# An attention kernel with a mixture-of-experts tail: q and k transposes placed apart between score steps, the two heads of a pair attended apart, the loads of the start and of V rearranged

## Chip, cores and metric

One core of a Trainium2 chip. The metric is the time on the device in microseconds (us) of one execution, lower is better. A profiled execution shows a span, from its first to its last instruction, about 2 us below that time. Single executions of this kernel spread by 2 to 3% (207.68 to 212.74 us before the change). A run is called slow when it is over 1.5% above the fastest of the same kernel, and verdicts use the fast runs; a verdict is "unclear" when the interval of the ratio includes a change of 2%.

## The reference

Causal attention over 64 (batch, head) groups, with 16 unmasked "beacon" keys and values ahead of the 576 tokens, then a soft mixture of experts on the result. Cut to what matters:

```python
B, H, S, Nb, D = 8, 8, 576, 16, 64
k_all = concat([beacon_k, k], axis=2); v_all = concat([beacon_v, v], axis=2)
scores = q @ k_all^T / sqrt(D)           # causal on the 576, beacons open
a = softmax(scores)
x = (a @ v_all)  ->  [4608, 512]
logits = x @ phi                         # 32 slots
slot_input = softmax over tokens(logits).T @ x
slot_out[e] = relu(slot_input[e] @ w1[e]) @ w2[e]      # 8 experts
out = softmax over slots(logits) @ slot_out
```

## The kernel before

The work goes over 32 pairs of heads, four pairs a batch. For each pair PE (matmul) transposes q and k into `qT`, `kT`. It makes the scores in four steps and ACT (ScalarE) turns each into exp. POOL (GpSimd) masks the diagonal. PE attends (exp times V), and DVE (VectorE) normalizes. V of a batch arrives as rows in `vbuf`, which has two buffers, and DVE turns it into `vh` with two stream transposes. The tail (logits of the last batch, experts, output) takes about 50 us. POOL issues the loads that cast to f16: V in four quarters, the beacon V rows on top of the first quarter, and the expert weights. The queue of SP (SyncE) issues q and k.

In the traces here each engine takes up its work in the order of the program (below, DVE stands idle for 3.68 us ahead of a V transpose, with a q copy behind it whose transposes PE has finished), so where a piece stands in the loop body decides what waits behind it. Four small pieces of the mixture of experts are spread over the pairs too: `xt_piece` transposes the attended result into `xT`, `logit_piece` multiplies it by phi and ACT takes exp, `dt_piece` transposes those exps into `dT`, and `add_si` adds to the slot inputs. They use the same two transpose buffers `tr`. The body for pair `n` (`b`, `g` are its batch and its place in it), cut:

```python
def transp(n):                      # 18 + 18 PE transposes, each 18 into one of TWO tr buffers
    for (f, dst) in ((qf, qT[n % 3]), (kf, kT[n % 3])):
        tp = ps_tr.tile([P, J, 64], BF, name="tr", tag="tr")
        ...                         # PE transposes
        nc.vector.tensor_copy(out=dst..., in_=tp...)       # DVE frees tr
def stage(m): transp(m); load_pair(m + 5)

for n in range(NP):
    score(n, 0); score(n, 1)
    ...                             # starts of pairs 0 and 1 cut
    xt_piece(n - 2); attend(n - 1)  # attend: both heads, 30 matmuls, then normalize on DVE
    score(n, 2)
    stage(n + 2)                    # q and k transposes together
    score(n, 3)
    if g == 1: logit_piece(b - 1, 0)                       # and (b - 1, 1) for g == 2,
    ...                                                    # dt_piece g == 3, add_si g == 0
    if b >= 1 and b < B - 1 and g >= 2:
        turn_v(b + 1, g - 2)        # DVE: half of the next batch's V transpose
    if n >= 4 and b + 2 < B:
        load_v(b + 2, g)            # a quarter of V
        if g == 3: load_bv(b + 2)   # its 16 KB of beacon V, over quarter 0
    want = ... 14 * (n - 2) // 15 ...                      # weight loads
```

The softmax here doesn't subtract the row's maximum and nothing guards it: scores larger than these inputs give would overflow.

## Time and profile before

Three runs gave a median of 209.36 us (207.68 to 212.74). The profiled span is 205.7 us. From the timeline of ACT I read when the first exp of each pair starts, which divides the span:

| stretch | us |
|---|---|
| start, to the first exp of pair 6 | 40.4 |
| pairs 6 to 31 (first exp to first exp), 25 periods | 115.7, that is 4.63 each |
| from there to the end | 49.6 |

The page of the kernel before: busy time by engine, then three rows of 40 equal slices (granted PE clock in tenths, busy share of the DMA engines in tenths, GB/s landed).

```profile
span 205.7 us, 7788 instructions
...
PE 153.0 (74%) x3409; PEld 113.3 (55%) x3409; DVE 134.7 (65%) x278; ACT 126.8 (62%) x188; POOL 93.6 (46%) x184
...
PEclk9999999999999969999997899999999999999755
DMA  5999979699999999999999999999999920079996
GB/s 177 328 222 353 255 225 242 116 243 248 259 261 255 260 265 262 259 263 256 261 341 267 261 294 267 251 246 215 212 213 208 213 56 3 0 304 409 419 422 280
```

No engine is full, but the DMA row stands at 9 from about 40 us until 165. V and weights land as f16, half their bytes in memory, so the GB/s row understates what is read (the page counts 50.88 MB moved, but 62.69 MB read from memory and 9.44 MB written).

The waits of the kernel before over the whole span (who waited for whom: us in total, times, longest us); the prediction quotes them between 30 and 150 us, where they are a little smaller:

```profile
ACT ex L263 <- PE sc L257: 29.7, 29, 4.7
...
ACT eLh L324 <- PE tr L320: 8.5, 12, 0.8
...
PE tr L320 <- DVE qT L245: 6.8, 11, 0.7
...
PE tr L332 <- DVE qT L245: 3.7, 6, 0.8
```

ACT waits for PE. PE waits where a logits or a dT piece needs one of the two transpose buffers while DVE still copies q and k, one behind the other.

The 16 KB of beacon V, line of the source query, with the time from issue to landing:

```profile
L146 POOL DMA_DIRECT2D vbuf<-in_beacon_v_dram x7: 521/521/552, 25.3 to 124.0; - x7
...
DMA to landing us min/median/max: 3.3/6.7/9.2
```

And this is where it stands in time for batch 4, in the timeline (start us, us, engine, line, what): issued by POOL during pair 11, used by DVE at the end of pair 14.

```profile
66.33 0.52 POOL L146 DMA_DIRECT2D vbuf<-in_beacon_v_dram  x1
...
81.31 0.75 DVE L245 COPY kT<-tr 128x576 bf16<-128x576 bf16 x1
...
81.97 1.14 DVE L135 STREAM_TRANSPOSE vh<-vbuf 128x512 f32<-128x512 f32 x1
...
82.97 1.11 DVE L135 STREAM_TRANSPOSE vt<-arena 96x512 f32<-96x512 f32 x1
```

The load is issued 15.6 us ahead of the V transpose that needs it. No V transpose waits in the loop.

### The profile page before, as it was taken

The page shows a single profiled execution, that of the slowest core. Times are in us where ns is not written, and L with a number is a line of the kernel's source. Part 1 is how long each engine was busy: PE and PEld are TensorE (multiplying, and loading weights), DVE is VectorE, ACT ScalarE, POOL GpSimd, SP SyncE. Part 2 cuts the span into 40 slices and gives each one's busy share as a digit, 9 for nine tenths or more (in the row PEclk, how much of TensorE's full clock was granted, in tenths as well). Part 3 has the DMA queues.
Part 4 walks back from the last instruction along what each step waited for, and adds up shares of the span by engine and source line. Part 5 has one row for each costly group of instructions (what it writes and reads, how often), then busy time and mean ns, then how long its engine had stood idle before and what let it go on. Part 6 is the DMA issues. An engine that isn't in the chain of part 4 may idle for free.

```text
span 205.7 us, 7788 instructions
## 1 busy us (share of the span) xinstructions
PE 153.0 (74%) x3409; PEld 113.3 (55%) x3409; DVE 134.7 (65%) x278; ACT 126.8 (62%) x188; POOL 93.6 (46%) x184
## 2 busy tenths in 40 slices
PE   2654798888778698878887987888878998788100
PEld 1433676667656586756666666667656664333000
DVE  4507969679658858976794689678655541299300
ACT  2560578588677658858884787688679122299200
POOL 5657372868675644644583467445457000000000
PEclk9999999999999969999997899999999999999755
DMA  5999979699999999999999999999999920079996
GB/s 177 328 222 353 255 225 242 116 243 248 259 261 255 260 265 262 259 263 256 261 341 267 261 294 267 251 246 215 212 213 208 213 56 3 0 304 409 419 422 280
DMA packets 20273, 50.88 MB, mean 247 GB/s; under 512 B 5392, under 2 KB 5392, under 8 KB 19216
## 3 DMA queue, kind: packets, MB, share of 16 engines
q0 software_dynamic: 8000, 21.75, 54.1%
q1 hardware_dynamic: 12096, 28.35, 38.2%
q8 instruction: 26, 0.43, 0.8%
q10 hardware_dynamic: 144, 0.29, 0.4%
q14 instruction: 7, 0.06, 0.1%
HBM read 62.69 MB, written 9.44 MB: 351 GB/s over the span
## 4 chain that ended last, share of the span: by engine, by line
PE 38%; DVE 36%; DMA 8%; issue 7%; ACT 2%; POOL 2%; DVEq 0%; ACTq 0%; POOLq 0%
PE av L284 12%; DVE xb L295 9%; DVE qT L245 8%; PE sc L257 7%; DMA vbuf<-in_v_dram 5%; DVE arena L569 5%; DVE vh L135 4%; PE tr L320 4%; PE tr L309 4%; DVE kT L245 4%; DMA vbuf<-in_beacon_v_dram 2%; PE tr L243 2%; DVE r L294 2%; PE av L537 2%; PE tr L343 2%
## 5 line engine op out<-in xcount | busy, mean ns | idle before, releaser
L263 ACT ACTIVATE ex<-sc 128x1024 f16<-128x1024 f32 (+1 forms) x124 | 100.8, 871 | 30.2 <-PE sc L257 29.7
L265 POOL TENSOR_SCALAR_AFFINE_SELECT ex<-ex 128x1024 f16<-128x1024 f16 x31 | 34.0, 1096 | 51.6 <-ACT ex L263 51.6
L257 PE MATMUL sc<-qT,kT 64*128 64x128 bf16 (+5 forms) x576 | 42.7, 255 | 4.2 <-issue 1.3
L284 PE MATMUL av<-vh,ex 128*128 128x65 f16 x868 | 37.1, 200 | 1.2 <-DVE vh L135 0.6
L284 PEld LDWEIGHTS <-ex 128*128 128x128 f16 x930 | 35.8, 109 | 2.6 <-issue 2.3
L243 PE MATMUL tr<-idb,arena 64*64 64x64 bf16 x1152 | 28.2, 202 | 10.3 <-DVE qT L245 5.0
L243 PEld LDWEIGHTS <-arena 64*64 64x64 bf16 x1152 | 23.9, 116 | 18.1 <-issue 15.9
L295 DVE TENSOR_TENSOR xb<-av,r 128x640 f16<-128x640 f32 (+1 forms) x33 | 26.5, 804 | 1.1
L257 PEld LDWEIGHTS <-kT 64*128 64x128 bf16 (+1 forms) x576 | 19.5, 99 | 12.9 <-issue 7.5
L245 DVE COPY qT<-tr 128x576 bf16<-128x576 bf16 x32 | 23.9, 748 | 2.4 <-PE tr L243 2.2
L245 DVE COPY kT<-tr 128x576 bf16<-128x576 bf16 x32 | 24.0, 749 | 1.4 <-PE tr L243 1.4
L313 DVE COPY xT<-tr 128x592 f16<-128x592 f16 x32 | 14.4, 455 | 12.9 <-PE tr L309 12.8
L135 DVE STREAM_TRANSPOSE vh<-vbuf 128x512 f32<-128x512 f32 x16 | 18.1, 1134 | 6.8 <-DMA arena<-in_v_dram 6.8
L164 POOL DMA_DIRECT2D arena<-in_moe_w_dram x32 | 17.6, 552 | 0.1
L111 POOL DMA_DIRECT2D vbuf<-in_v_dram x28 | 15.7, 566 | 3.5 <-DVE xT L313 3.5
L294 DVE RECIPROCAL r<-av 128x10 f32<-128x10 f32 (+1 forms) x33 | 7.2, 218 | 15.1 <-PE av L284 15.1
L320 PE MATMUL tr<-xT,phih 128*128 128x288 f16 x56 | 9.1, 284 | 6.9 <-DVE qT L245 6.8
L309 PE MATMUL tr<-idh,xb 128*128 128x128 f16 (+1 forms) x160 | 13.9, 220 | 0.3 <-DVE xb L295 0.3
L569 DVE TENSOR_SCALAR arena<-fp,rc 128x512 f32<-128x512 f32 x18 | 12.3, 746 | 0.7 <-PE fp L565 0.7
L565 PE MATMUL fp<-soh,eLh 128*128 128x512 f16 x36 | 10.5, 377 | 2.6 <-ACT arena L567 1.4
L567 ACT ACTIVATE arena<-fp,rc 128x512 f32<-128x512 f32 x18 | 11.3, 685 | 1.7 <-PE fp L565 1.0
L309 PEld LDWEIGHTS <-xb 128*128 128x128 f16 (+1 forms) x160 | 9.2, 98 | 5.5 <-issue 4.8
(83 smaller groups left out, 135.6 us busy)
## 6 DMA issues: line engine op xcount, KB each, us to landing
arena<-in_moe_w_dram POOLq DMA_DIRECT2D x32, 512.0 KB, 10.2
arena<-in_q_dram SPq DMA_DIRECT2D x32, 288.0 KB, 10.1
arena<-in_k_dram SPq DMA_DIRECT2D x31, 288.0 KB, 12.2
out_dram<-arena SPq DMA_DIRECT2D x8, 1024.0 KB, 8.5
vbuf<-in_v_dram POOLq DMA_DIRECT2D x31, 128.0 KB, 7.3
out_dram<-arena SPq DMA_DIRECT2D x2, 512.0 KB, 3.1
arena<-in_v_dram POOLq DMA_DIRECT2D x4, 128.0 KB, 9.9
arena<-in_k_dram ACTq DMA_DIRECT2D x1, 288.0 KB, 2.8
```

The costliest lines, as they stand in the source:

```text
L135: nc.vector.transpose(out=dst[:, e], in_=src.bitcast(FP).rearrange("p (j e) -> p e j", j=TK)[:, e])
L164: nc.gpsimd.dma_start(out=arena[:, wloc[m]:wloc[m] + WP], in_=src)
L243: nc.tensor.transpose(tp[po:po + 64, j, :], hi, idb[po:po + 64, po:po + 64])
L245: nc.vector.tensor_copy(out=dst[:, Nb:Nb + S].rearrange("p (s j) -> p s j", j=J), in_=tp[:, :, :].rearrange("p j s -> p s j"))
L257: nc.tensor.matmul(sc[0:kn, a, col:col + un], kT[n % 3][64 * a:64 * a + 64, P * c:P * c + kn], qT[n % 3][64 * a:64 * a + 64, u0:u0 + un], ...
L263: nc.scalar.activation(ex[n][:, :, o:o + w], sc[:, :, 0:w], AF.Exp, scale=scale)
L265: nc.gpsimd.affine_select(out=ex[n][:, :, 0:512].rearrange("p a (c t) -> p a c t", c=4), in_=ex[n][:, :, 0:512].rearrange("p a (c t) -> p ...
L284: nc.tensor.matmul(av[0:m, a, i * DD:(i + 1) * DD], ex[n][0:kn, a, o:o + m], vchunk(b, 2 * g + a, c, kn), start=(c == 0), stop=(c == i))
L295: nc.vector.tensor_tensor(out=xo[:, z], in0=avv[:, z, :, 0:D], in1=r_.unsqueeze(3).broadcast_to([P, z.stop - z.start, NCH, D]), op=AL.mult)
L309: nc.tensor.transpose(tp[:, i, 0:m], xb[b % 2][0:m, i, 2 * g:2 * g + 2, :].rearrange("p h d -> p (h d)"), idh[0:m, 0:m])
L320: nc.tensor.matmul(lp[:, 0:w], phih[:, t, :, :].rearrange("p g s -> p (g s)"), xT[b][:, t, Nb + hf * w:Nb + (hf + 1) * w], start=(t == 0), ...
L569: nc.vector.tensor_scalar(out=osb[:, j, :], in0=fp_[:, :], scalar1=rc[:, i:i + 1], scalar2=None, op0=AL.mult)
```

## The change

The intent: spread PE's work evenly between score steps, so that ACT never waits long for a score. q is transposed between steps 1 and 2 and k between 2 and 3; one head is attended ahead of step 2 and the other behind step 3. The V transposes move up to between steps 0 and 1. At the start, later loads are held back so that the first V lands sooner. V and beacon V loads from batch 3 on come later, and so do most weight loads. The exp tile's layout changes too. The core of the diff, cut:

```diff
+    def hold(n):                       # a tiny DVE write that delays the load over it
+        o = lend + 2 * (n % QKS) * 2 * J * D
+        nc.vector.memset(arena[0:1, o:o + 2], 0.0)
 ...
-    load_pair(2)
-    load_pair(3)
-    nc.sync.dma_start(out=bkf[:, 1:B, :], in_=bks[:, 1:B, :])
-    load_pair(4)                       # these now behind hold(2), and hold(3) at the end of pair 0
-    double_beacons(nc.gpsimd, 1, 0, 1) # now on DVE
 ...
     for n in range(NP):
         score(n, 0)
+        if n == 1:
+            turn_v(0, 0)
+        if n in (3, 4):
+            turn_v(1, n - 3)
+        if 1 <= b < B - 1 and g >= 2:
+            turn_v(b + 1, g - 2)
         score(n, 1)
-            attend(n - 1)
+        if m < NP:
+            transp(m, 0)                # q
+            attend_head(n - 1, 0)
+                xt_piece(x)
         score(n, 2)
-            stage(n + 2)
+            transp(m, 1)                # k
         score(n, 3)
+            attend_head(n - 1, 1)
+            normalize(n - 1)
 ...
-        if n in (3, 4):
-            turn_v(1, n - 3)
-        if b >= 1 and b < B - 1 and g >= 2:
-            turn_v(b + 1, g - 2)
-        if n >= 4 and b + 2 < B:
-            load_v(b + 2, g)
-            if g == 3:
-                load_bv(b + 2)
+        if n >= 5:
+            x, y = divmod(n - 5, 4)
+            if x + 3 < B:
+                load_v(x + 3, y)
+            if y == 0 and 3 <= x + 2 < B:
+                load_bv(x + 2)          # at the end of the pair just before its V transpose
-        want = 0 if n < 3 else 14 * (n - 2) // 15 if n < 24 else 19 + 7 * (n - 23) // 4
+        want = 7 * max(n - 1, 0) // 10 if n < 24 else 16 + 9 * (n - 23) // 5
```

More of the change, by code (lines that the diff above doesn't have):

```diff
@@ L67 @@
                 if u0 <= lo < u0 + un:
-                    blk[(c, i)] = soff[st] + col + lo - u0
+                    blk[(c, i)] = (2 * soff[st] + col + lo - u0, width[st])
     assert len(blk) == 15
@@ L178 @@
     load_pair(1)
-    load_pair(2)
-    load_pair(3)
-    nc.sync.dma_start(out=bkf[:, 1:B, :], in_=bks[:, 1:B, :])
-    load_pair(4)
     phif = const.tile([P, NDC, NSL], FP, name="phif")
-    nc.sync.dma_start(out=phif[:, :, :], in_=moe_phi.rearrange("(c p) e -> p c e", p=P))
     idb = const.tile([P, P], BF, name="idb")
@@ L233, in beacons, with transp @@
                     "p b (g r n) -> p (b g) r n", g=H // 2, r=2)[:, :, r, :])
-    def transp(n):
-        (nc.vector if n < 2 else nc.gpsimd).tensor_copy(out=kT[n % 3][:, 0:Nb], in_=bkT[:, n, :])
-        for (f, dst) in ((qf, qT[n % 3]), (kf, kT[n % 3])):
-            t = f.pop(n)
-            tp = ps_tr.tile([P, J, 64], BF, name="tr", tag="tr")
-            for j in range(J):
-                for po in (0, 64):
-                    hi = t[po:po + 64, j, :].bitcast(BF)[:, 1::2]
-                    nc.tensor.transpose(tp[po:po + 64, j, :], hi,
-                                        idb[po:po + 64, po:po + 64])
-            nc.vector.tensor_copy(out=dst[:, Nb:Nb + S].rearrange("p (s j) -> p s j", j=J),
-                                  in_=tp[:, :, :].rearrange("p j s -> p s j"))
+    def transp(n, i):
+        if i == 1:
+            (nc.vector if n < 2 else nc.gpsimd).tensor_copy(out=kT[n % 3][:, 0:Nb],
+                                                            in_=bkT[:, n, :])
+        t = (qf, kf)[i].pop(n)
+        tp = ps_tr.tile([P, J, 64], BF, name="tr", tag="tr")
+        for j in range(J):
+            for po in (0, 64):
+                hi = t[po:po + 64, j, :].bitcast(BF)[:, 1::2]
+                nc.tensor.transpose(tp[po:po + 64, j, :], hi, idb[po:po + 64, po:po + 64])
+        nc.vector.tensor_copy(
+            out=(qT, kT)[i][n % 3][:, Nb:Nb + S].rearrange("p (s j) -> p s j", j=J),
+            in_=tp[:, :, :].rearrange("p j s -> p s j"))
     ex = {}
@@ L251, in score @@
         if st == 0:
-            ex[n] = (arena[:, 20 * WP:20 * WP + 2 * EW].rearrange("p (a w) -> p a w", a=2)
-                     if n == 2 else exq.tile([P, 2, EW], F16, name="ex", tag="ex"))
+            ex[n] = (arena[:, 20 * WP:20 * WP + 2 * EW] if n == 2 else
+                     exq.tile([P, 2 * EW], F16, name="ex", tag="ex"))
         sc = scs[st % 2]
@@ L261, in score @@
                     start=True, stop=True)
-        w, o = width[st], soff[st]
-        nc.scalar.activation(ex[n][:, :, o:o + w], sc[:, :, 0:w], AF.Exp, scale=scale)
+        w = width[st]
+        e = ex[n][:, 2 * soff[st]:2 * soff[st] + 2 * w].rearrange("p (a w) -> p a w", a=2)
+        nc.scalar.activation(e, sc[:, :, 0:w], AF.Exp, scale=scale)
         if st == 0:
-            nc.gpsimd.affine_select(
-                out=ex[n][:, :, 0:512].rearrange("p a (c t) -> p a c t", c=4),
-                in_=ex[n][:, :, 0:512].rearrange("p a (c t) -> p a c t", c=4),
-                compare_op=AL.is_ge, fill=0.0, base=0,
-                pattern=[[0, 2], [0, 4], [1, P]], channel_multiplier=-1)
@@ L270, in score @@
-        if st == 1:
-            nc.gpsimd.affine_select(
-                out=ex[n][0:UL, :, o:o + UL], in_=ex[n][0:UL, :, o:o + UL],
-                compare_op=AL.is_ge, fill=0.0, base=0,
-                pattern=[[0, 2], [1, UL]], channel_multiplier=-1)
-    def attend(n, split=False):
-        b, g = divmod(n, H // 2)
-        for a in range(2):
-            for i in range(NCH):
-                m = P if i < 4 else UL
-                for c in range(i + 1):
-                    kn = P if c < 4 else UL
-                    o = blk[(c, i)]
-                    nc.tensor.matmul(
-                        av[0:m, a, i * DD:(i + 1) * DD],
-                        ex[n][0:kn, a, o:o + m],
-                        vchunk(b, 2 * g + a, c, kn),
-                        start=(c == 0), stop=(c == i))
+            e4 = e.rearrange("p a (c t) -> p a c t", c=4)
@@ new lines, in score, with attend_head @@
+            nc.gpsimd.affine_select(out=e4, in_=e4, compare_op=AL.is_ge, fill=0.0, base=0,
+                                    pattern=[[0, 2], [0, 4], [1, P]], channel_multiplier=-1)
+        if st == 1:
+            e1 = e[0:UL, :, 0:UL]
+            nc.gpsimd.affine_select(out=e1, in_=e1, compare_op=AL.is_ge, fill=0.0, base=0,
+                                    pattern=[[0, 2], [1, UL]], channel_multiplier=-1)
+    def attend_head(n, a):
+        b, g = divmod(n, H // 2)
+        for i in range(NCH):
+            m = P if i < 4 else UL
+            for c in range(i + 1):
+                kn = P if c < 4 else UL
+                o, w = blk[(c, i)]
+                nc.tensor.matmul(
+                    av[0:m, a, i * DD:(i + 1) * DD],
+                    ex[n][0:kn, o + a * w:o + a * w + m],
+                    vchunk(b, 2 * g + a, c, kn),
+                    start=(c == 0), stop=(c == i))
@@ L289, in attend, with normalize @@
+    def normalize(n, split=False):
+        b, g = divmod(n, H // 2)
         r5 = sml.tile([P, 2, NCH], FP, name="r5", tag="r5")
@@ L353, in add_si, with load_more @@
         nc.vector.tensor_tensor(out=z, in0=z, in1=sp, op=AL.add)
-    def stage(m):
-        transp(m)
+    def load_more(m):
         if m + 5 < NP:
             load_pair(m + 5)
-    double_beacons(nc.vector, 0, 0, 1)
+    for r in range(2):
+        double_beacons(nc.vector, r, 0, 1)
     beacons(0, 1)
-    stage(0)
+    transp(0, 0)
+    transp(0, 1)
+    hold(2)
+    load_pair(2)
     nc.vector.tensor_copy(out=idh[:, :], in_=idb[:, :])
@@ L367 @@
         score(n, 0)
-        score(n, 1)
-        if n == 0:
-            stage(1)
-        elif n == 1:
-            turn_v(0, 0)
-            stage(2)
+        if n == 1:
[4 more added lines that the diff above has]
+            turn_v(b + 1, g - 2)
+        if 13 <= n < 15:
+            turn_tail(1, n - 13)
+        score(n, 1)
+        m = n + 1 if n < 4 else n + 2
+        if m < NP:
+            transp(m, 0)
+        if n in (2, 3):
+            attend_head(n - 2, 0)
+        elif n > 3:
+            attend_head(n - 1, 0)
+        if n >= 3:
+            for x in {3: (0,), 4: (1, 2)}.get(n, (n - 2,)):
+                xt_piece(x)
+        score(n, 2)
+        if n == 3:
+            beacons(1, B)
+        if m < NP:
+            transp(m, 1)
+            if n > 0:
+                load_more(m)
+        score(n, 3)
+        if n == 0:
+            hold(3)
+            load_pair(3)
+            nc.sync.dma_start(out=bkf[:, 1:B, :], in_=bks[:, 1:B, :])
+            load_pair(4)
+            nc.sync.dma_start(out=phif[:, :, :], in_=moe_phi.rearrange("(c p) e -> p c e", p=P))
+            load_more(0)
+            load_more(1)
+        if n == 1:
             turn_v(0, 1)
@@ L376 @@
             turn_tail(0, 1)
-            for r in range(2):
-                double_beacons(nc.gpsimd, r, 1, B)
-        elif n <= 3:
-            attend(n - 2)
-        else:
-            for m in ((n - 2,) if n > 5 else (2 * n - 8, 2 * n - 7)):
-                xt_piece(m)
-            attend(n - 1)
-        score(n, 2)
-        if n == 2:
-            beacons(1, B)
-        if 2 <= n < NP - 2:
-            stage(n + 2)
-        score(n, 3)
-        if n == 1:
-            stage(3)
-        if n == 3:
-            attend(2)
-        if n >= 5 and g == 1:
-            logit_piece(b - 1, 0)
-        if n >= 6 and g == 2:
-            logit_piece(b - 1, 1)
+        if n in (2, 3):
+            attend_head(n - 2, 1)
+            normalize(n - 2)
+        elif n > 3:
+            attend_head(n - 1, 1)
+            normalize(n - 1)
+        if n == 3:
+            attend_head(2, 0)
+            attend_head(2, 1)
+            normalize(2)
+            transp(5, 0)
+            transp(5, 1)
+            load_more(5)
         if n >= 6 and g == 3:
             dt_piece(b - 1)
+        if n >= 5 and g in (1, 2):
+            logit_piece(b - 1, g - 1)
         if n >= 8 and g == 0:
@@ L405 @@
         if n == 1:
+            for r in range(2):
+                double_beacons(nc.gpsimd, r, 1, B)
             for qd in range(4):
@@ L420 @@
                 load_v(2, qd)
-        if n >= 4 and b + 2 < B:
-            load_v(b + 2, g)
-            if g == 0 and b == 1:
-                load_bv(2)
-            if g == 3:
-                load_bv(b + 2)
+        if n == 4:
+            load_bv(2)
+        if n >= 5:
[4 more added lines that the diff above has]
+                load_bv(x + 2)
         if 8 <= n < 11:
             load_tail(1, n - 8)
-        if 13 <= n < 15:
-            turn_tail(1, n - 13)
-        want = 0 if n < 3 else 14 * (n - 2) // 15 if n < 24 else 19 + 7 * (n - 23) // 4
+        want = 7 * max(n - 1, 0) // 10 if n < 24 else 16 + 9 * (n - 23) // 5
         while wl < min(want, NPC):
@@ L434 @@
             wl += 1
+    while wl < NPC:
+        load_w(wl)
+        wl += 1
     G = 4
@@ L461 @@
     xt_piece(NP - 2)
-    attend(NP - 1, split=True)
+    attend_head(NP - 1, 0)
+    attend_head(NP - 1, 1)
+    normalize(NP - 1, split=True)
     lps = [scs[0][:, hf, 0:S // 2] for hf in range(2)]
```

## The prediction

> **What bounds it now.** Three unprofiled runs give a median of 209.36 us (207.68 to 212.74); the profiled span is 205.7. First exp of each pair in the timeline: pair 2 at 20.2, pair 6 at 40.4, pair 31 at 156.1. So start-up is 40 us, then 25 pairs at 4.63 us, then 50 us of tail that the change hardly touches. In the pair loop no engine is full: ACT needs 3.5 us a pair (exps 3.15, logits 0.3); DVE about 3.7 (q and k copies 0.7 each, normalize 1.04, xT 0.45, half a V transpose 0.55, small ones); PE back to back about 3.7 (scores 1.05, attend 1.2, transposes 0.68, xT 0.26, logits, slots). PE's order paces it: in the waits between 30 and 150 us ACT waits 23.3 us for scores and 8.5 for logits, PE 13 us for the transpose buffers that DVE's q and k copies free, and several "issue" stalls of over 1 us. The windows show a DMA share of 1.03 to 1.08 from 40 to 165 us: V and weight loads land 6 to 12 us after issue.
>
> **The change** removes and adds no arithmetic. It moves half the attend and half the transposes into other gaps between score steps: PE's longest stretch without a score falls from 1.45 us (xT plus attend) to about 1.2, and the k copy no longer queues directly behind the q copy, so the 0.65 us wait of each logits group and 0.5 of each dT group should mostly go. I work out 3.8 to 4.05 us a pair, plus 0.2 for issue stalls and throttle: 4.2. Over 25 pairs: -11 us.
>
> Start-up: V of batch 0 landed only at 16.4 us, and DVE idled 6.8 us before its first V transpose. Holding pair 2 and later back, and freeing POOL of the beacon cast, should land V near 10 us: -5. But batch 1's V beacons are now needed at the start of pair 3, not its end (before: issued 25.3, landed 30.4, on the chain). I keep -2.5 us.
>
> Added wait: from batch 3 on, a batch's beacon V is issued one pair before its V transpose (three before), behind a V load in the same queue. It leaves POOL 0.6 to 1 us before DVE wants it, yet the trace lands these 16 KB loads 3.35 to 9.2 us after issue. DVE stalls there with all copies behind it, five times. The Trainium skill (DMA: Bandwidth & Descriptors, Anatomy of one DMA) gives about 2 us fixed cost; the trace's least is 3.35. Fewer early weight loads (7 in ten pairs, before 14 in 15) shorten the queue. I charge 1.5 us net each: +7.5; it could be 3.
>
> All issuers share 16 DMA engines (same page, Issuing engines are not separate DMA queues; the share above 1 agrees); 62.7 MB read at about 410 GB/s forbids much under 190 us.
>
> Sum: 209.4 - 11 - 2.5 + 7.5 = about 203 us; 8 in 10 between 195 and 212. Chances: faster 0.54, same 0.32, slower 0.14.
>
> **What would show it.** Pair period 4.1 to 4.3 where no V transpose waits; PE's waits for transpose buffers under 5 us; first V transpose at 10 to 11 us; V transposes waiting 2 to 4 us for beacon V at pairs 3, 10, 14, 18, 22, 26; last weights landing without holding the experts.
>
> **What would make it wrong.** Beacon V landing faster in an emptier queue (then 192 to 196), each stall costing its full 3 to 5 us (then 210 or more), or DVE becoming the bound through V transposes ahead of the q copy.

## The result and the profile after

The changed kernel takes 237.06 us (234.92 to 237.53, 4 runs). The ratio to the kernel before is 1.1354, 95% interval 1.1247 to 1.1460. A ratio here is the mean time of one kernel's fast runs over that of the other's fast runs of the same rounds, so it is not quite the ratio of the quoted medians. The forecast of 203 us, with 212 as its upper end, was wrong.

The profiled spans, divided as before:

| stretch | before | after | difference | predicted |
|---|---|---|---|---|
| start, to the first exp of pair 6 | 40.4 | 47.8 | +7.4 | -2.5 |
| pairs 6 to 31 | 115.7 | 135.6 | +19.9 | -3.5 (-11 and +7.5) |
| from there to the end | 49.6 | 51.5 | +1.9 | 0 |
| span | 205.7 | 234.9 | +29.2 | -6 |

Of the +1.9 us at the end, 1.2 lie in the last pair itself, where the second head is now attended behind the last score step; the rest was not followed up.

The page after, with the line of the chain that ended last:

```profile
span 234.9 us, 7781 instructions
...
PE 169.6 (72%) x3409; PEld 123.4 (53%) x3409; DVE 139.0 (59%) x281; ACT 126.9 (54%) x188; POOL 93.4 (40%) x183
...
PEclk9999999999795997699769955995599999999955
DMA  6899729999999899779949983999999999029996
GB/s 203 188 337 344 182 57 173 252 263 228 260 208 225 202 246 182 181 191 220 208 110 224 248 192 104 203 229 211 188 179 208 194 212 197 8 101 416 419 423 250
...
DMA vbuf<-in_beacon_v_dram 14%; PE av L280 13%; PE sc L256 9%; PE tr L242 8%; ACT ex L263 4%; DVE vh L139 4%; DVE arena L597 3%; DVE qT L243 3%; DMA arena<-in_beacon_k_dram 3%; DMA vbuf<-in_v_dram 3%; PE tr L319 2%; PE tr L308 2%; DVE xb L294 2%; POOL ex L266 2%; PE av L565 2%
```

Busy times of ACT and POOL are as before, and DVE has 4 us more. What grew is idle time and PE's busy time at a lower clock: the clock row, nearly all 9 before, now has a group of 5 to 7 every 20 us or so. And the chain spends 14% of the span on a 16 KB load.

The waits after, over the whole span:

```profile
ACT ex L263 <- PE sc L256: 60.7, 32, 6.0
...
DVE vh L139 <- DMA vbuf<-in_beacon_v_dram: 24.9, 5, 5.8
PE tr L242 <- DVE qT L243: 24.9, 7, 6.1
...
DVE vh L139 <- DMA arena<-in_v_dram: 3.9, 2, 3.2
```

DVE waits 24.9 us for beacon V in five places (one at the start, four in the loop), plus once 3.2 us (pair 10) that the trace puts down to the V tail's load. The landing times say that this wait too ends with beacon V: in all five loop pairs that load lands 0.1 to 0.5 us before the V transpose starts (69.28 and 69.47 us in pair 10). PE's wait for DVE's q copy is, by chance, also 24.9 us. ACT's wait for scores rises from 29.7 to 60.7. The load itself has not become slower, as its source query shows:

```profile
L150 POOL DMA_DIRECT2D vbuf<-in_beacon_v_dram x7: 537/549/549, 25.8 to 154.3; - x7
...
  DVE vh L139: 24.9, 5
...
DMA to landing us min/median/max: 3.6/5.1/7.0
```

Before, 3.3 to 9.2 us from issue to landing; now 3.6 to 7.0. What changed is when it is wanted. The same batch 4 as above, in the timeline after:

```profile
86.53 0.54 POOL L150 DMA_DIRECT2D vbuf<-in_beacon_v_dram  x1
...
87.09 0.82 DVE L294 TENSOR_TENSOR xb<-av,r 128x640 f16<-128x640 f32 x1
...
89.03 0.37 PE L256 MATMUL sc<-qT,kT 64*128 64x464 bf16 x2
...
91.59 1.12 DVE L139 STREAM_TRANSPOSE vh<-vbuf 128x512 f32<-128x512 f32 x1 [3.68 <-DMA vbuf<-in_beacon_v_dram]
92.58 1.07 DVE L139 STREAM_TRANSPOSE vt<-arena 96x512 f32<-96x512 f32 x1
93.50 0.73 DVE L243 COPY qT<-tr 128x576 bf16<-128x576 bf16 x1
...
94.29 0.69 PE L242 MATMUL tr<-idb,arena 64*64 64x64 bf16 x18 [4.89 <-DVE qT L243]
...
95.20 1.00 PE L280 MATMUL av<-vh,ex 128*128 128x65 f16 x14
95.31 0.52 ACT L263 ACTIVATE ex<-sc 128x416 f16<-128x416 f32 x1 [4.81 <-PE sc L256]
```

Read it downwards. POOL issues the load at 86.5. DVE is done with normalize at 87.9 and wants the V transpose at once, 1.4 us after the issue instead of 15.6. It starts at 91.59, 3.68 us idle. The q copy is behind it, and behind another transpose. PE did its q transposes, half an attend, xT and score step 2 (89.03), and then stands before the k transposes. These need one of the two transpose buffers, and the q copy has to free it: 4.89 us idle. ACT gets no score for 4.81 us. When PE resumes, 18 transposes take 0.69 us and 14 attend matmuls 1.00; the same groups of 18 and 14 took 0.47 and 0.63 at 87.77 and 88.17. Two windows show why, the first being this pair (us, busy us and instructions of PE, PEld, DVE, ACT, POOL, then granted clock, DMA share, GB/s), the second the next three pairs:

```profile
core 0: us, PE busy (x) PEld busy (x) DVE busy (x) ACT busy (x) POOL busy (x), PEclk, DMA share, GB/s
87.75:97.88 10.13, 5.24 (x95) 3.92 (x93) 5.48 (x9) 3.76 (x7) 2.57 (x5) 0.67 0.97 201
97.88:109.57 11.69, 11.43 (x300) 8.96 (x296) 9.88 (x21) 10.06 (x14) 7.64 (x15) 1.00 0.75 172
```

The granted clock is 0.67 in the stalled pair and 1.00 after it. The Trainium skill (TensorE: Matmul & The Clock Gate, Part 1) says that PE falls to half clock after an idle window of about 3.4 us and needs about as long busy to get back. The trace agrees in part: its clock records show 0.5 six times ahead of the output phase, once for 3.4 us and five times for 6.8 or 10.2 us. These five begin 1.8 to 3.8 us after PE went idle in each of the five stalls and end 3.7 to 6.5 us after PE resumed (here from 91.2 to 98.0). A whole idle window was not needed: the sixth record, at 60.4 us, and two in the kernel before, at 73.5 and 111.1, follow 3.4 us in which PE was busy for 2.23, 1.79 and 1.79 us and never idle for more than 1.4 at a time.

The five pairs that hold such a wait (10, 14, 18, 22, 26) last 8.69, 10.13, 9.83, 11.31 and 10.90 us, together 50.9; before, the same five took 22.8. The other twenty pairs take 84.7 us, 4.24 each; before, 92.9, or 4.65 each. So the loop lost 28.0 us in five pairs and won 8.2 in twenty. Counted as the prediction's sum counts, against the 4.24 us of the other pairs, the five cost 29.7 us more, 5.9 each.

### The profile page after: what moved, and what is told of

It reads as the page before. It is cut to its first block, busy times and chain, and to the rows that moved or that the text cites. A ratio compares the mean times of both kernels' runs of the same rounds, so it can differ in the third digit from the quotient of the medians.

```text
span 234.9 us, 7781 instructions
## 1 busy us (share of the span) xinstructions
PE 169.6 (72%) x3409; PEld 123.4 (53%) x3409; DVE 139.0 (59%) x281; ACT 126.9 (54%) x188; POOL 93.4 (40%) x183
## 4 chain that ended last, share of the span: by engine, by line
PE 43%; DMA 21%; DVE 15%; ACT 5%; issue 4%; POOL 4%; DVEq 1%; SPq 0%; ACTq 0%
DMA vbuf<-in_beacon_v_dram 14%; PE av L280 13%; PE sc L256 9%; PE tr L242 8%; ACT ex L263 4%; DVE vh L139 4%; DVE arena L597 3%; DVE qT L243 3%; DMA arena<-in_beacon_k_dram 3%; DMA vbuf<-in_v_dram 3%; PE tr L319 2%; PE tr L308 2%; DVE xb L294 2%; POOL ex L266 2%; PE av L565 2%
## 5 line engine op out<-in xcount | busy, mean ns | idle before, releaser
L263 ACT ACTIVATE ex<-sc 128x1024 f16<-128x1024 f32 (+1 forms) x124 | 100.3, 871 | 61.9 <-PE sc L256 60.7
L242 PE MATMUL tr<-idb,arena 64*64 64x64 bf16 x1152 | 35.0, 211 | 29.6 <-DVE qT L243 24.9
L242 PEld LDWEIGHTS <-arena 64*64 64x64 bf16 x1152 | 28.8, 123 | 43.9 <-issue 34.8
L256 PE MATMUL sc<-qT,kT 64*128 64x128 bf16 (+5 forms) x576 | 46.6, 277 | 4.3 <-ACT ex L263 1.7
L280 PE MATMUL av<-vh,ex 128*128 128x65 f16 x868 | 43.9, 208 | 0.3
L280 PEld LDWEIGHTS <-ex 128*128 128x128 f16 x930 | 40.3, 115 | 5.5 <-issue 1.6
L139 DVE STREAM_TRANSPOSE vh<-vbuf 128x512 f32<-128x512 f32 x16 | 18.1, 1130 | 28.8 <-DMA vbuf<-in_beacon_v_dram 24.9
L243 DVE COPY kT<-tr 128x576 bf16<-128x576 bf16 x32 | 24.2, 757 | 10.0 <-PE tr L242 9.8
L256 PEld LDWEIGHTS <-kT 64*128 64x128 bf16 (+1 forms) x576 | 21.3, 108 | 15.4 <-issue 8.1
L312 DVE COPY xT<-tr 128x592 f16<-128x592 f16 x32 | 14.7, 459 | 7.5 <-PE tr L308 6.2
L308 PE MATMUL tr<-idh,xb 128*128 128x128 f16 (+1 forms) x160 | 15.2, 231 | 1.5 <-DVE xb L294 0.9
L115 POOL DMA_DIRECT2D vbuf<-in_v_dram x28 | 15.6, 560 | 0.0
L308 PEld LDWEIGHTS <-xb 128*128 128x128 f16 (+1 forms) x160 | 11.1, 107 | 2.0 <-DVE xb L294 1.3
L319 PE MATMUL tr<-xT,phih 128*128 128x288 f16 x56 | 11.7, 341 | 0.0
```

The lines of the kernel that those rows point to most:

```text
L139: nc.vector.transpose(out=dst[:, e], in_=src.bitcast(FP).rearrange("p (j e) -> p e j", j=TK)[:, e])
L242: nc.tensor.transpose(tp[po:po + 64, j, :], hi, idb[po:po + 64, po:po + 64])
L243: nc.vector.tensor_copy(out=(qT, kT)[i][n % 3][:, Nb:Nb + S].rearrange("p (s j) -> p s j", j=J), in_=tp[:, :, :].rearrange("p j s -> p s j"))
L256: nc.tensor.matmul(sc[0:kn, a, col:col + un], kT[n % 3][64 * a:64 * a + 64, P * c:P * c + kn], qT[n % 3][64 * a:64 * a + 64, u0:u0 + un], ...
L263: nc.scalar.activation(e, sc[:, :, 0:w], AF.Exp, scale=scale)
L280: nc.tensor.matmul(av[0:m, a, i * DD:(i + 1) * DD], ex[n][0:kn, o + a * w:o + a * w + m], vchunk(b, 2 * g + a, c, kn), start=(c == 0), sto ...
```

## The experiments

Theory A: the beacon V load, issued one pair ahead and wanted right behind normalize, makes the loss of the loop. Rival B: the new order of PE and DVE is itself bad (V transposes ahead of the q copy, attend in halves), and another wait would take the place of this one. Four kernels on one chip, where the kernel before took 209.07.

**e1_bv_early**: the changed kernel, beacon V issued two pairs earlier, all else kept.

```diff
-            if y == 0 and 3 <= x + 2 < B:
-                load_bv(x + 2)
+            if y == 2 and x + 3 < B:
+                load_bv(x + 3)
```

> The changed kernel with one edit: from batch 3 on, the beacon V of a batch is issued two pairs earlier (three pairs ahead of its V transpose, as before the change); everything else stays. Theory A (the late beacon V is the loss of the pair loop: five pairs of 8.7 to 11.3 us against about 4.2): those five pairs fall to 4.2 to 5.2 us, the last V quarter still being issued one pair ahead; time 208 to 214 us against 237, so within 2% or slightly over the kernel before. Rival B (the new order on PE and DVE is what costs, and another wait takes the place of this one): still over 225 us.

Measured: 215.61 us, ratio 1.0298 (1.0235 to 1.0360). One moved 16 KB load takes most of the loss away. It is 1.6 us over what I gave it: in three of the five pairs the V transpose still waits 1.2 to 1.8 us, now that the last V quarter is the late one (issued two pairs ahead, not one as I had written; for pair 10 at 57.6 us, landed at 65.1, wanted at 63.9), and pairs 10 and 14 still take 7.0 and 7.6 us.

**e2_v_as_before**: the V quarters also one pair earlier, so the V load timing of before.

```diff
-        if n >= 5:
-            x, y = divmod(n - 5, 4)
-            if x + 3 < B:
-                load_v(x + 3, y)
-            if y == 0 and 3 <= x + 2 < B:
-                load_bv(x + 2)
+        if n >= 4 and b + 2 < B:
+            load_v(b + 2, g)
+            if g == 3:
+                load_bv(b + 2)
```

> The changed kernel with the whole V load timing of before from batch 3 on (V quarters one pair earlier, beacon V two pairs earlier). Theory A: as e1 or 1 to 3 us better, 206 to 212 us, with no V transpose waiting for a DMA after pair 6, and the pair period 4.0 to 4.3. What is left over the kernel before is then the start, where the first exp of pair 6 is 7.5 us later. Rival B: over 225 us.

Measured: 211.79 us, ratio 1.0094 (1.0008 to 1.0179). No V transpose waits after pair 6. The pair period of 4.0 to 4.3 us did not come: it is 4.52 here and 4.48 in s3 below. (The profile of e2 fell in a slow run, so I take sizes of the loop from s3, which is fast.)

**e3_turn_late**: the late loads kept, the V transposes back at the end of the pair.

```diff
         score(n, 0)
-        if 1 <= b < B - 1 and g >= 2:
-            turn_v(b + 1, g - 2)
 ...     # behind attend, normalize, logits, dT:
+        if 1 <= b < B - 1 and g >= 2:
+            turn_v(b + 1, g - 2)
```

> The changed kernel with its late V and beacon V loads, but the V transposes from batch 2 on back at the end of the pair, behind normalize, where they stood before. Theory A: beacon V lands 5 to 7 us after issue and now has about 4 us more, so the five waits shrink from 5 us to 1 to 2 us and stand behind the q, k and xT copies: 211 to 219 us. Rival B: over 225 us.

Measured: 214.10 us, ratio 1.0220 (1.0151 to 1.0289). Two of the waits are left, 0.7 and 1.6 us, and the loop takes 112.5 us instead of 135.6.

**e4_before_bv_late**: the kernel BEFORE with only these two pieces put in.

```diff
         score(n, 0)
+        if b >= 1 and b < B - 1 and g >= 2:
+            turn_v(b + 1, g - 2)
         score(n, 1)
 ...
-            if g == 3:
-                load_bv(b + 2)
+        if b >= 2 and g == 1 and b + 1 < B:
+            load_bv(b + 1)
```

> The kernel BEFORE, with only the two pieces that theory A blames put in: beacon V issued one pair ahead from batch 3 on, and the V transposes from batch 2 on between the first two score steps. Transposes, attend, start and weights stay as before. Theory A: 20 to 30 us slower than before (229 to 239 us), with five pairs of 9 to 11 us. Rival B: within 4 us of before.

Measured: 236.34 us, ratio 1.1248 (1.1144 to 1.1353), almost the whole loss of the change, in the old kernel. The same five pairs take 12.7, 10.3, 10.1, 10.0 and 6.8 us (the last below my 9 to 11, the first above). The whole loss is in the loop, 141.3 us instead of 115.7, while start and end are as before. The trace names beacon V as the releaser of two of the five waits only, but in all five the load lands 0.02 to 0.2 us before the V transpose starts. The timeline of DVE in this run has the same line:

```profile
90.97 1.12 DVE L135 STREAM_TRANSPOSE vh<-vbuf 128x512 f32<-128x512 f32 x1 [4.83 <-DMA vbuf<-in_beacon_v_dram]
```

What follows: A holds and B falls, in both directions. Either edit taken back (e1, e3) gives most of the time back, because each alone leaves the load a lead of 5.0 us or more, from its issue to the moment when DVE wants it; the two together leave 1.2 to 2.1 us in the changed kernel and 0.8 to 1.8 in e4. The new exp layout and weight timing were not taken apart, but e1 to e3 keep the layout and the weight timing, and their loops are no longer than before (112.5 to 114.6 us against 115.7).

Next, the start, 7.4 us later than before. Theory H: the holds. Theory T: batch 1's V transpose, now ahead of the copies of pair 3, waits for its beacon V with the work of that pair behind it. The timeline of DVE in the changed kernel shows that wait:

```profile
29.56 1.13 DVE L139 STREAM_TRANSPOSE vh<-vbuf 128x512 f32<-128x512 f32 x1 [5.76 <-DMA vbuf<-in_beacon_v_dram]
```

This load is late in itself: POOL issues it at 25.8 us, about 2 us after DVE wants it, having stood idle for 2.3 us until a V load landed, and it lands 3.7 us after issue.

Before, the first exps of pairs 3 and 4 came at 26.0 and 30.5 us; in the changed kernel at 24.2 and 39.0. So pair 3 came 1.7 us earlier and then lost 10.3. The holds are not shown to have brought it forward: without them it comes at 23.3 (s1, s3), and e4, with the start of before, has it at 24.7. Three kernels on another chip, where before took 211.42. All start from e2.

**s1_no_hold**: without the holds.

```diff
+    load_pair(2); load_pair(3); bkf load; load_pair(4); phif load      # at once, as before
-    hold(2); load_pair(2)
-            hold(3); load_pair(3); bkf load; load_pair(4); phif load
```

> The kernel of e2 (V load timing of before) and also the q, k, beacon and phi loads of the start issued at once as before, without the two holds. Theory H (the holds cost the start: pair 2 lands at 13.4 us, and the k beacons, which POOL must cast before it issues batch 1's V, only at 18.1 us): the first exp of pair 6 comes 3 to 6 us earlier than the 47.7 us of e2, time 206 to 209 us. Theory T (what costs is the V transpose of batch 1 put ahead of the copies of pair 3, with DVE idle 5.8 us and the work of three pairs behind it): within 2 us of e2, 210 to 213 us.

Measured: 211.98 us, ratio 1.0003 (0.9904 to 1.0102). The first exp of pair 6 is at 47.1, against 47.7 in e2. The holds do bring the first V transpose forward (14.7 us here, 11.2 in the changed kernel), but nothing was gained by it at pair 6. DVE's waits in the first 40 us still have the line:

```profile
DVE vh L139 <- DMA vbuf<-in_beacon_v_dram: 5.1, 1, 5.1
```

**s2_turn1_late**: holds kept, batch 1's two V transposes back at the end of pairs 3 and 4.

```diff
         score(n, 0)
-        if n in (3, 4):
-            turn_v(1, n - 3)
 ...     # end of the pair
+        if n in (3, 4):
+            turn_v(1, n - 3)
```

> The kernel of e2 with batch 1's two V transposes back at the end of pairs 3 and 4, holds kept. Theory T: pair 4's first exp moves from 38.9 to 31 to 34 us, time 204 to 208 us. Theory H: little change, 210 to 213 us.

Measured: 208.89 us, ratio 0.9870 (0.9795 to 0.9945); pair 4 begins at 33.4 instead of 38.9, pair 6 at 43.9 instead of 47.7. So T holds for 5.5 us at pair 4 and 3.8 at pair 6, about half of the 7.4 us; the rest goes with the edits of s3 and s4 below. The time is 0.9 us above my range, and the verdict against the kernel before is unclear by the 2% rule.

**s3_both**: both edits.

> The kernel of e2 with both start edits. If both theories hold in part, 202 to 206 us, faster than before by 1.5 to 3%; the loop stays at 4.4 to 4.55 us a pair because pauses for PE instructions (gaps of about 1 us ending some 1.4 us after an instruction packet, 15 us in the loop of e2, 7 before) eat what the order gains. If only the loop of e2 counts and neither start edit does: 210 to 213 us.

Measured: 207.64 us, ratio 0.9809 (0.9725 to 0.9892), a little above the range I gave in us, on a chip where the kernel before was slower too; by the 2% rule this is unclear as well. Pair 4 begins at 32.0, pair 6 at 42.5. With and without holds the intervals overlap (s1 and e2, s3 and s2), so what the holds cost or save is not settled; it is 2 us at most in these medians.

**c1_warm_in_wait**, same chip: the changed kernel with dummy matmuls where PE waits, to see what the fallen clock is worth.

```diff
+        if 2 <= b < B - 1 and g == 2:
+            for _ in range(45):                       # into unused columns of av
+                nc.tensor.matmul(av[:, 0, NCH * DD:512], idh[:, :],
+                                 xT[b - 1][:, 0, 0:512 - NCH * DD], start=True, stop=True)
         if m < NP:
             transp(m, 1)
```

> The changed kernel with 45 dummy matmuls of 187 columns (about 4 us) put on PE just ahead of the k transposes of the five pairs in which PE waits for DVE, writing unused columns of the attend banks. Nothing else changes. Theory C (part of each loss is PE's granted clock falling to 0.5 while it waits and for about 3 us after: 18 transposes 0.69 instead of 0.47 us, half an attend 1.00 instead of 0.63): the clock stays at 1.0 there, and each such pair is 1 to 1.5 us shorter, 229 to 233 us. If the clock plays no part, or DVE sets the pace after the wait: 236 to 239 us.

Measured: 231.38 us, ratio 1.0987 (1.0872 to 1.1103) against 1.1354 for the changed kernel: more matmuls, less time. The window of pair 14 of this run (columns as above) has the clock at 1.00:

```profile
87.02:94.56 7.54, 7.54 (x140) 6.45 (x138) 4.87 (x8) 3.68 (x7) 2.57 (x5) 1.00 0.99 216
```

The five pairs take 43.6 us instead of 50.9. In this profile DVE's waits before them sum to 20.8 us instead of 22.3, so 1.5 of the 7.3 us are not the clock's; the rest is about 1.2 us a stall, an average over pairs that differ: they are 0.7 to 2.6 us shorter, DVE waited only 1.9 us in the pair shown, and the clock stayed at 1.00 in four of the five (in pair 22 it fell to 0.5 for 3.4 us). The low clock of the changed kernel lasted 3.7 to 6.5 us after PE resumed, longer than the 3 us of the expectation.

Last, where the gain of the new order goes once the stalls are gone. In s3 the loop takes 112.1 us, 3.6 less than before, and not the 11 that I had forecast. The PE timeline of e2 shows a kind of gap that waits for nothing that the profile shows:

```profile
107.03 0.22 PE L308 MATMUL tr<-idh,xb 128*128 128x128 f16 x1
108.56 0.38 PE L308 MATMUL tr<-idh,xb 128*128 128x128 f16 x4 [1.30 <-issue]
```

In the middle of five equal transposes PE stops for 1.3 us. The trace also has the packets of the queue that carries instructions, 16 KB each, and one ended at 107.00. I counted gaps of PE's weight loads of 0.35 us or more that end 1.1 to 1.7 us behind the end of such a packet: 8 with 7.6 us in pairs 6 to 31 before, 13 with 12.5 us in s3, and 1 with 1.3 us in the changed kernel, whose stalls presumably leave PE time to be supplied. (e2's profile is of a slow run, but s3, with the thirteen, is fast.) Theory F: those packets come late because the DMA engines are crowded by weights, q, k and V. Two kernels, one look each (state unknown), with all weight loads issued behind the loop; the results are still correct, only the loop is to be compared.

**d1_s3_weights_after** and **d2_before_weights_after**:

```diff
-        want = ...
+        want = 0                    # in the kernel before: the weight loop moved behind the pair loop
```

> The kernel of s3 with all 32 weight loads issued after the pair loop (still correct; the whole must get some 60 to 80 us longer, only the loop counts). Theory F (in s3 thirteen PE pauses, 12.5 us in pairs 6 to 31, wait for instruction packets that the crowded DMA engines deliver late): the pauses fall under 3 us and the loop from 4.48 to 3.85 to 4.0 us a pair. If the pauses have another cause: loop still 4.3 to 4.5.

> The kernel BEFORE with all weight loads issued after the loop. Theory F and the order of the change being really better: pauses gone here too (7.6 us before), loop 4.63 to 4.2 to 4.35, so with the DMA engines free the new order of PE is worth 0.3 to 0.45 us a pair against it. If the new order is worth nothing by itself: the same loop as d1 within 0.1.

The whole takes 259.32 and 268.56 us, as it must. The windows of pairs 6 to 31, first s3, then d1, then d2 (columns as above):

```profile
42.50:154.60 112.10, 98.88 (x2393) 76.16 (x2392) 89.23 (x168) 85.98 (x128) 65.69 (x128) 0.97 1.02 242
```

```profile
42.70:142.90 100.20, 94.31 (x2393) 74.48 (x2391) 87.93 (x168) 85.06 (x127) 51.30 (x101) 1.00 0.59 147
```

```profile
43.00:152.20 109.20, 91.59 (x2393) 73.48 (x2391) 86.29 (x167) 85.02 (x128) 51.07 (x101) 1.00 0.52 135
```

The DMA share falls from 1.02 to 0.59 and 0.52, the pauses to 0.8 us (one) and 1.9 us (three), and the loop from 112.1 to 100.2 us in the new order (4.01 a pair, a hair over my range) and from 115.7 to 109.2 in the old (4.37, also a hair over). So the changed kernel without its stalls is worth about 9 us of loop with free DMA engines and 3.6 with crowded ones; I put this down to the order of PE, which was not changed by itself. The largest waits of PE that the old order keeps are those for transpose buffers, here of d2; the new order has 3.3 us of waits for the q copy in d1:

```profile
PE tr L320 <- DVE qT L245: 7.8, 12, 0.7
PE tr L332 <- DVE qT L245: 4.1, 6, 0.9
PE tr L343 <- DVE qT L245: 3.9, 6, 0.7
```

This shows that taking the weights away takes the pauses away. That the late instruction packets cause them is a reading of their timing, not shown by itself.

**s4_start2**: a try for a faster kernel, s3 with two more edits at the start.

```diff
             attend_head(n - 2, 0)
+            if n == 3:
+                attend_head(1, 1)
+                normalize(1)          # and no longer behind score(3, 3)
 ...
         if n == 1:
+            for qd in range(4):
+                load_v(1, qd)
             for r in range(2):
                 double_beacons(nc.gpsimd, r, 1, B)
-            for qd in range(4):
-                load_v(1, qd)
```

> A try for a faster kernel: s3, with pair 1 attended whole in one place in pair 3 as before the change (s3 left PE 1.4 us idle there on normalize), and batch 1's V loads issued ahead of the beacon cast on POOL, which had held them to 18.2 us. Expected: pair 4 begins 1 to 3 us earlier than the 32.0 of s3, time 204 to 207 us where before takes 209, ratio 0.965 to 0.98. If DVE, not the loads, sets the start: as s3, 0.98.

Measured: 204.71 us (201.89 to 207.07, 6 runs, three of them called slow), where the kernel before took 209.96; ratio 0.9685 (0.9603 to 0.9767). Pair 4 begins at 30.3 and pair 6 at 40.8, nearly as before (40.4). This beats both kernels; its interval overlaps that of s3. The two edits were not taken apart.

## Why the prediction was wrong

1. **The charge for beacon V was mis-sized; this is the step that failed.** The prediction put it so: "I charge 1.5 us net each: +7.5; it could be 3." In the terms of that sum it measured +29.7 us, 5.9 each (28.0 against the same pairs before). The wait itself was foreseen at the right pairs, as "2 to 4 us"; it was 3.2 to 5.8 us, 22.3 in sum. What was wrong is "net": I took half of it as hidden. Nothing hides it, because DVE does the q copy only behind the V transpose, and that copy frees the transpose buffer that PE needs 1.7 to 1.8 us into the pair. PE idled 3.3 to 6.1 us in the five pairs, 24.4 in sum. On top come the two things that the prediction did not have: PE's clock at 0.5 until 3.7 to 6.5 us after PE resumes, some 1.2 us a stall (c1), and the V transposes themselves, which then run while PE waits (1.9 us in pair 14). e1, e3 and e4 confirm the cause.

2. **The start had the wrong sign.** "I keep -2.5 us"; it was +7.4. The first V transpose came at 11.2 us, just past the forecast 10 to 11, but s1 shows that this bought nothing at pair 6. And the transpose of batch 1 waited 5.76 us at the head of pair 3, and in pair 3 that holds back the copies of pair 4 and, behind them, two normalizes and pair 5's transposes. Before, the same load landed at 30.4 with that work already done. s2 gives 5.5 us back at pair 4, and 3.8 at pair 6, by moving this one piece; the rest goes with the edits of s3 and s4 (pair 6 at 42.5 and 40.8), of which no single one is shown to be the cause.

3. **The order on PE was right in kind.** "I work out 3.8 to 4.05 us a pair, plus 0.2 for issue stalls and throttle: 4.2." The twenty undisturbed pairs take 4.24. But that the number held was in part luck: with the stalls gone (s3) the loop is at 4.48 and 12.5 us of PE pauses are there, against 1.3 in the changed kernel, and only without weight loads does it reach 4.01. That the stalls emptied the DMA queues, so that the pauses stayed away, fits (DMA share 0.75 behind the stall of pair 14) but is not shown. By s3, the term of -11 us would have been about -3.6 by itself.

4. "PE's waits for transpose buffers under 5 us" failed with the stalls (24.9 us), and no wait of the experts for their last weights appeared, as forecast.

I had named the right outcome among those that would make the prediction wrong ("each stall costing its full 3 to 5 us (then 210 or more)") and given it too little weight.

## What to carry to other kernels

Before a load or its use is moved, work out the lead, from the issue on its queue to the moment when the engine that needs it arrives; if it is below the slowest landing that the trace shows for that load (here 9.2 us), count the whole difference as lost. A waiting instruction costs everything placed behind it on its engine: ask which buffer that work frees and who stops for it (here PE, 24.4 us in five pairs), and add the slow clock of a matmul engine left idle (here 0.5 until 3.7 to 6.5 us after stalls of 3.3 to 6.1 us). A small load needs as much lead as the queue it stands in (here 3.3 to 9.2 us for 16 KB), and moving it two pairs earlier was worth more here than the whole reordering around it.

## What the Trainium skill lacked or had wrong

- Runtime: NRT & Kernel Launch, Instruction fetch mechanics, says that instructions stream in 16 KiB blocks of 256 over a DMA queue and that crossing a block is "mostly hidden". The block size agrees (16 KB packets). The pauses that follow such packets cost 7.6 us of the loop before and 12.5 us in s3 while the DMA engines were full, and 0.8 to 1.9 us without the weight loads; the page does not say that crowded DMA engines matter here. That the packets themselves cause the pauses is not shown.
- DMA: Bandwidth & Descriptors, Anatomy of one DMA, gives about 2 us of fixed cost plus the bytes at 436 GB/s for a DMA from POOL, which is an estimate of 2.04 us for 16 KB. Here such loads took 3.3 to 9.2 us before and 3.6 to 7.0 after; the page's sum has no term for what is queued ahead.
- TensorE: Matmul & The Clock Gate tells to avoid PE idle gaps over about 3 us. The five stalls agree, but gaps well under 3 us were enough elsewhere: three records of 0.5 (before at 73.5 and 111.1 us, after at 60.4) follow 3.4 us with no PE gap over 1.4 us and PE busy for 1.79 to 2.23 us. The runs also add a remedy with its size that the page does not list for such waits: dummy matmuls where PE waits kept the clock at 1.00 in four of the five stalls (c1, DVE waits of 1.9 to 6.1 us) and saved about 1.2 us a stall on average.
